# Attention ahead of a channel mix on one core: the second product of a head on quarters of TensorE, in whole float32

## The chip, the cores and the metric

One core of one Trainium2 chip runs the whole kernel. The metric is the device time of one execution in microseconds (us), the median of several runs.

## What is computed

Attention over 8 batches with 8 heads of 64, 576 queries, and keys and values averaged over pools of 8 (72 pooled keys); its output, put together to rows of 512, goes through a channel mix with a token shift.

```python
k_p = k.reshape(B, H, Sp, pool, D).mean(axis=3)      # Sp = 72, pool = 8, D = 64
v_p = v.reshape(B, H, Sp, pool, D).mean(axis=3)
scores = scale * np.matmul(q, k_p.transpose(0, 1, 3, 2))
attn = softmax(scores)
x = np.matmul(attn, v_p)                              # then (B, 576, 512)
x_prev = x one token earlier, zeros at a batch's start
xk = mu_k * x + (1.0 - mu_k) * x_prev                 # xr likewise with mu_r
k = np.maximum(xk @ w_k, 0.0)                         # 512 -> 1024
v = k * k @ w_v                                       # 1024 -> 512
r = 1.0 / (1.0 + np.exp(-(xr @ w_r)))                 # 512 -> 512
return (r * v).astype(np.float32)
```

The weights arrive as 64-bit floats, and the kernel makes float32 of them itself.

## The kernel before, in words

The 4608 tokens are 12 chunks of 384, and each chunk is three tiles of 128 tokens. A batch has 576 tokens, so chunks 1, 4, 7 and 10 lie over two batches, with 192 tokens of each; the other eight lie within one. `units` and `stretches` (L393) hold this.

For a tile, `softmax` (L676) makes the scores with 16 small matmuls (L698): 64 rows of the array by 64 columns, so that four of them, one on each quarter of the array, belong together. The softmax follows on DVE, ACT and POOL. In chunks 0 and 1 the weights of a tile are transposed by TensorE (`transposed` L813, `transposed_rest` L871); from chunk 2 on DVE turns blocks of 32 (`turned` L771), a DMA puts them in DRAM, and `fetch_turned` (L798) brings a chunk of them back, keys on the partitions, to the one buffer `turned_sb`.

`attended` (L901) is attention's second product. Two heads make a group g, four groups make a chunk. The 64 first keys of both heads lie on the 128 partitions; the values of both heads stand on the diagonal of one 128 x 128 matrix (`vbd_h`, `vbd_l`, made by `values` L616). But for chunk 0, whose product is in whole float32, weights and values are split into a rounded part and the rest (`pth`, `ptl`, made by `split_turned` L843 on ACT and DVE), and three matmuls give the product. A fourth, `ptr` with `vbd_r`, adds the 8 last keys. So a group is four matmuls of 384 columns, or eight of 192 where the chunk lies over two batches. Then the same thread makes the shifted rows: ACT writes `t` (L944), POOL copies one column from or to `carry` (L951, L953), and DVE makes `xm` (L964). A thread `x_parts` (L976), added at that point, splits `xm` on ACT (L980) and POOL (L982) into `xkh`, `xkl`, `xrh`, `xrl`.

`hidden` (L986) is the first layer: 8 output blocks of a chunk, each over four blocks of input `ct`, which are the four groups, with three matmuls each (one in chunk 0). `gate` (L1043) is the sigmoid's product, `mixed` (L1072) the last one: three tiles of 24 matmuls of 512 columns. `attended` of a chunk may begin when the gate of the chunk before it is done, so it stands among the matmuls of that chunk's `mixed`.

The order of all instructions is made when the program is written. Each piece of work is a generator that yields an engine and a planned length; the class `Order` holds a planned clock for each engine and takes, on the engine that can start first, the thread with the smallest due time. Due times come from the table `DUE`, found for this order, or from formulas. `LOADS` is the order of the first DMAs, and tables such as `SUM_BY`, `NORM_BY` and `LOW_BY` name the engine of sums over the pool, of the softmax's scaling and of the split of weights. A thread starts with the planned time 0:

```python
self.at, self.pe_at, self.step, self.last = 0.0, None, None, None
```

so a step of a thread that another thread adds midway can be planned earlier than the step that feeds it. Sums over the pool on POOL are three instructions at L578 (`halve`), on TensorE eight at L589 (`summed`).

Of the kernel before, what the change touches and what calls it, by code (L numbers as in the profile page):

```python
# [8 lines left out]
F32 = mybir.dt.float32  # L9
F32R = mybir.dt.float32r  # L10
# [35 lines left out]
SUM_BY = {"k0": "t", "k1": "v", "v0": "t", "v1": "t", "r0": "t", "k2": "t", "k3": "t", "v2": "g", "v3": "g", "r1": "v", "k5": "v", "k4": "v", "v5": "v", "r2": "v", "v4": "v"}

NORM_BY = {0: "v", 1: "v", 2: "v", 3: "v", 7: "g", 5: "g", 4: "v", 8: "v", 6: "v"}
WARMING = 4
# [1162 lines left out]
```

## Time and profile before

| | |
|---|---|
| median of 3 runs | 617.71 us (617.42 to 619.48) |
| the profiled execution | 618.18 us, span 616.3 us |
| mean granted clock of TensorE | 0.994 of full |
| PE busy | 600.9 us (97%) |
| DVE, ACT, POOL busy | 406.1, 359.6, 195.7 us |
| DMA | 68.73 MB, 37% of 16 engines' span |

The span is from the first to the last instruction; the execution's own time is 1.88 us longer. PE is the matrix engine, DVE the vector engine, ACT the scalar engine. The ends of matmuls are modelled, so the distance from one start to the next says more than a single duration. A product in whole float32 shows as two records in the trace, a split one as one record for each matmul.

### The profile page before, as it was taken

To read this page: it belongs to the slowest core of one execution; us is meant where nothing else is said; L and a number is where in the kernel's file an instruction comes from. 1 tells how busy PE (TensorE), PEld (TensorE's weight loads), DVE (VectorE), ACT (ScalarE), POOL (GpSimd) and SP (SyncE) were. 2 spreads that over 40 slices of the span, in tenths; PEclk is the share of its full clock that TensorE was granted. 3 is DMA by queue.
4 is the path that set the end of the run, shared out by engine and by line. 5 is a ranking of instruction groups with operands and counts; after the bars stand their busy time and mean duration, and the time that the engine had idled before them with its cause. 6 is when DMAs were issued, how large, how long until landed. Compare 5 with 4: busy or idle time off the path is not lost.

```text
span 616.3 us, 10622 instructions
## 1 busy us (share of the span) xinstructions
PE 600.9 (97%) x3948; PEld 509.3 (83%) x3948; DVE 406.1 (66%) x834; ACT 359.6 (58%) x761; POOL 195.7 (32%) x282
## 2 busy tenths in 40 slices
PE   7899999998999999999999999999999999999997
PEld 6755458887988988988988988988988988988985
DVE  5998969966766865984975854786885833623411
ACT  4999976764575766546646545665654643634420
POOL 1030373327205216425515105615523303304100
PEclk9999999999899999999999999999999999999999
DMA  9997122841358124156147123039215030000001
GB/s 293 394 360 233 43 89 77 204 155 52 77 182 199 45 81 105 60 163 167 36 178 178 54 70 95 19 131 225 68 40 130 19 78 34 18 1 35 18 1 51
DMA packets 59460, 68.73 MB, mean 112 GB/s; under 512 B 11664, under 2 KB 43664, under 8 KB 59408
## 3 DMA queue, kind: packets, MB, share of 16 engines
q1 hardware_dynamic: 59264, 67.91, 37.1%
q8 instruction: 31, 0.51, 0.4%
q14 instruction: 21, 0.17, 0.1%
q10 hardware_dynamic: 144, 0.13, 0.1%
HBM read 49.75 MB, written 18.28 MB: 110 GB/s over the span
## 4 chain that ended last, share of the span: by engine, by line
PE 87%; POOL 4%; DVE 3%; DMA 3%; ACT 2%; issue 1%; SPq 0%; DVEq 0%; POOLq 0%; ACTq 0%
PE mm L1092 31%; PE mm L1009 30%; PE mm L1061 17%; PE bank L938 5%; PE sc L698 3%; POOL stage L578 2%; DMA early_sl<-in_vm 1%; DMA stage<-in_vr 1%; POOL xkl L982 1%; POOL xrl L982 1%; ACT t L944 1%; PE mm L589 1%; DVE xm L964 1%; DVE sl L1037 1%; ACT xkh L980 1%
## 5 line engine op out<-in xcount | busy, mean ns | idle before, releaser
L1009 PE MATMUL mm<-xkh,w_k 128*128 128x384 f32 x704 | 182.4, 340 | 2.6 <-ACT xkh L980 2.6
L1092 PE MATMUL mm<-w_v,sh 128*128 128x512 f32 x528 | 170.3, 392 | 0.0
L1009 PEld LDWEIGHTS mm<-xkh,w_k 128*128 128x128 f32 x704 | 127.9, 190 | 4.4 <-ACT xkh L980 2.8
L1009 PE MATMUL mm<-xkl,w_k 128*128 128x384 f32 x352 | 119.3, 339 | 0.4
L1092 PEld LDWEIGHTS mm<-w_v,sh 128*128 128x128 f32 x528 | 99.2, 188 | 20.4
L1092 PE MATMUL mm<-w_v,sl 128*128 128x512 f32 x264 | 103.1, 390 | 0.0
L749 POOL TENSOR_TENSOR e<-e,sm 128x576 f32<-128x576 f32 x28 | 34.5, 1232 | 184.8 <-DVE sm L744 174.0
L944 ACT ACTIVATE t<-bank,om_sb 128x384 f32<-128x384 f32 x96 | 49.2, 580 | 61.0 <-PE bank L938 60.9
L1061 PE MATMUL mm<-w_r,xrh 128*128 128x512 f32 x264 | 84.0, 392 | 0.2 <-DVE rk L1029 0.2
L1035 ACT CAST sh<-rk 128x384 fp32r<-128x384 f32 x88 | 45.0, 513 | 62.7 <-DVE rk L1029 62.4
L964 DVE SCALAR_TENSOR_TENSOR xm<-bank,mu_sb,t 128x384 f32<-128x384 f32 x88 | 51.1, 612 | 39.7 <-POOL t L955 21.6
L1105 DVE TENSOR_TENSOR rs<-mm,rs 128x512 f32<-128x512 f32 (+1 forms) x37 | 24.8, 673 | 79.0 <-PE mm L1092 79.0
L1009 PEld LDWEIGHTS mm<-xkl,w_k 128*128 128x128 f32 x352 | 66.9, 190 | 1.9 <-POOL xkl L982 1.8
L1037 DVE TENSOR_TENSOR sl<-rk,sh 128x384 fp32r<-128x384 f32 x88 | 53.7, 612 | 19.8 <-ACT sh L1035 19.1
L982 POOL TENSOR_TENSOR xkl<-xm,xkh 128x384 fp32r<-128x384 f32 x44 | 45.8, 1041 | 65.0 <-ACT xkh L980 64.6
L1061 PEld LDWEIGHTS mm<-w_r,xrh 128*128 128x128 f32 x264 | 49.5, 188 | 11.0 <-DVE rk L1029 0.4
L1029 DVE SCALAR_TENSOR_TENSOR rk<-mm,rk 128x384 f32<-128x384 f32 x88 | 48.3, 549 | 13.7 <-ACT rk L1022 13.3
L1092 PEld LDWEIGHTS mm<-w_v,sl 128*128 128x128 f32 x264 | 49.6, 188 | 9.1
L1022 ACT ACTIVATE rk<-mm 128x384 f32<-128x384 f32 x88 | 43.0, 489 | 16.6 <-PE mm L1009 16.0
L1061 PE MATMUL mm<-w_r,xrl 128*128 128x512 f32 x132 | 51.5, 390 | 0.0
L982 POOL TENSOR_TENSOR xrl<-xm,xrh 128x384 fp32r<-128x384 f32 x44 | 45.6, 1036 | 2.3 <-ACT xrh L980 2.1
L578 POOL TENSOR_TENSOR stage<-stage 128x512 f32<-128x512 f32 (+5 forms) x51 | 43.5, 870 | 1.1
(126 smaller groups left out, 866.4 us busy)
## 6 DMA issues: line engine op xcount, KB each, us to landing
out<-rs SPq DMA_DIRECT2D x35, 256.0 KB, 2.0
passing<-pm SPq DMA_DIRECT2D x30, 288.0 KB, 2.8
qs<-in_qT SPq DMA_DIRECT2D x32, 256.0 KB, 4.2
stage<-in_kT SPq DMA_DIRECT2D x14, 576.0 KB, 4.7
turned_sb<-passing SPq DMA_DIRECT2D x40, 192.0 KB, 4.4
stage<-in_vm SPq DMA_DIRECT2D x14, 512.0 KB, 6.0
got_wk<-in_w_k SPq DMA_DIRECT2D x8, 512.0 KB, 9.1
got_wv<-in_w_v SPq DMA_DIRECT2D x8, 512.0 KB, 9.3
```

The source lines that it names most:

```text
L578: nc_eng.tensor_tensor(out=st[:, :, :w], in0=st[:, :, :w], in1=st[:, :, w:2 * w], op=ALU.add)
L749: eng.tensor_tensor(out=e, in0=e, in1=sm.broadcast_to([P, 2, 4, KEYS]), op=ALU.mult)
L944: nc.scalar.activation(out=t[:, m, 1:n + 1], in_=xp, func=AF.Copy, scale=om_sb[:, m, g:g + 1])
L964: nc.vector.scalar_tensor_tensor(out=xm[:, :n], in0=xp, scalar=mu_sb[:, m, g:g + 1], in1=t[:, m, :n], op0=ALU.mult, op1=ALU.add,)
L982: nc.gpsimd.tensor_tensor(out=lo, in0=xm[:, :n], in1=hi, op=ALU.subtract)
L1009: nc.tensor.matmul(out=hp, lhsT=w[:, o], rhs=x[:, ct, o_t], start=(ct == 0 and k == 0), stop=(ct == NCT - 1 and k == len(terms) - 1),)
L1022: nc.scalar.activation(out=rk[:, :n], in_=hp, func=AF.Relu)
L1029: nc.vector.scalar_tensor_tensor(out=rk[:, :n], in0=hp, scalar=0.0, in1=rk[:, :n], op0=ALU.max, op1=ALU.mult)
L1035: nc.scalar.copy(out=sh, in_=rk[:, :n])
L1037: nc.vector.tensor_tensor(out=operand("sl", c)[:, jt, o_t], in0=rk[:, :n], in1=sh, op=ALU.subtract)
L1061: nc.tensor.matmul(out=bank, lhsT=x[:, ct, o], rhs=w, start=(ct == 0 and k == 0), stop=(ct == NCT - 1 and k == len(terms) - 1),)
L1092: nc.tensor.matmul(out=bank, lhsT=s[:, o], rhs=w, start=(jt == 0 and k == 0), stop=(jt == NJT - 1 and k == len(terms) - 1),)
```

## The change

`attended` takes two groups at once (a, two in a chunk). The last keys' products come first, one on each of two banks. Then the 64 first keys follow without a split: for each of the four heads a matmul on one quarter of the array, 64 rows by 64 columns, weights and values in whole float32, added to the banks. From chunk 2 on TensorE reads the weights from the turned blocks directly. `split_turned` handles only the 8 last keys, for a whole chunk at once. What followed the product is a thread of its own, `shifted`, one for each group. The values are no longer put on a diagonal: `values` is one copy. There are two buffers of turned blocks, and heads 1 and 2 of each four change places in the layout.

The planner counts a change between whole and quarter matmuls (`CHANGE`), prefers on PE what stays in the present mode (`rank`, `STAY`), and starts an added thread at the time of what adds it. `DUE`, `LOADS` and the tables of engines are new.

```diff
 LOADS = (
-    "k0 k1 q0 wr3 q1 r0 q3 wk0 c0 q2 wk1 wv6 v1 k2 wk4 k3 q5 wv1 v0 wr2 wk3 wk2 v3 q4 wr0 v2 "
+    "k0 k1 q0 q2 q1 r0 c0 wk1 wk0 q4 q3 wr3 v0 k2 v1 wk4 wr2 v2 wv7 k3 q5 wk3 wk7 wr0 wk2 wv6 "
...
 DUE = {
-    "keys 0 0": 72.94, "values 0 0": -3.14, "keys 0 1": -79.49, "values 0 1": -66.31,
+    "keys 0 0": 360.51, "values 0 0": -73.7, "keys 0 1": -104.6, "values 0 1": 135.34,
...
+    CHANGE = {"quarters": 0.1, "whole": 0.25}
...
-        self.fresh.append(Thread(DUE.get(name, due), steps, spare, name))
+        t = Thread(DUE.get(name, due), steps, spare, name)
+        t.at = self.now
+        self.fresh.append(t)
...
+        stays = t.step[0] == "pe" and (t.step[3] if len(t.step) > 3 else "whole") == self.mode
+        return t.due - (STAY if stays else 0.0)
...
 def values(b, p):
-            nc.scalar.copy(out=(vbd_w if as_is else vbd_h[i])[r, gs, r], in_=o[r])
+        nc.scalar.copy(out=vs[b % 2][:, 2 * p:2 * p + 2], in_=o)
...
-    def split_turned(i):
+    def split_turned(c):
...
-        nc.scalar.copy(out=pt_h, in_=main)
-        nc.vector.tensor_tensor(out=pt_l, in0=main, in1=pt_h, op=ALU.subtract)
...
-    def attended(c, g, p):
+    def attended(c, a, p):
...
-        yield need(
-            "om", *[("rest", b) for b, *_ in segs],
-            *[("values" if as_is else "value parts", b, q) for b, *_ in segs for q in range(2)],
-        )
+        yield need("om", *[("rest", b) for b, *_ in segs], *[("values", b, a) for b, *_ in segs])
...
-        bank = yield take("bank")
-        t = yield take("t")
+        both = [(yield take("bank")), (yield take("bank"))]
...
-                vh, vl = vbd_h[i][:, g], vbd_l[i][:, g]
-                terms = [(vh, ph), (vl, ph), (vh, pl)]
-            terms.append((vbd_r[i][:, r, 2 * j:2 * j + 2, :], operand("ptr", c)[:, r, o]))
+        yield "pe", sum(2 * pe(k)[1] for _, _, k, _ in segs), False
...
+            for h2 in range(2):
                 nc.tensor.matmul(
+                    out=both[h2][:, at:at + k], lhsT=vbd_r[b % 2][:, a, 2 * h2:2 * h2 + 2, :],
+                    rhs=operand("ptr", c)[:, a, off + at:off + at + k], start=(q == 0), stop=False,
...
+        yield "pe", sum(pe(k, True)[1] for _, _, k, _ in segs), False, "quarters"
+        for q, (b, s, k, at) in enumerate(segs):
+            for j in range(2):
+                for h2 in range(2):
+                    r, to = slice(h2 * D, (h2 + 1) * D), both[h2][j * D:(j + 1) * D, at:at + k]
...
+                    nc.tensor.matmul(
+                        out=to, lhsT=vs[b % 2][r, 2 * a + j, :], rhs=pt, start=False, stop=True,
...
+        for h2 in range(2):
+            order.add(att_due[c] + 2 * a + h2, shifted(c, 2 * a + h2, p, both[h2]))
```

The order that comes of it is shown at three places. On PE, the last group of chunk 2 among the last matmuls of chunk 1's `mixed` (L1092, L1136 are `mixed`, `sc` are scores), before:

```order
L1092 MATMUL mm_118<-w_v_1135,sh_959 128x512
L938 MATMUL bank_117<-pth_1150,vbd_h_72 128x384
L938 MATMUL bank_117<-pth_1150,vbd_l_74 128x384
L938 MATMUL bank_117<-ptl_1151,vbd_h_72 128x384
L938 MATMUL bank_117<-ptr_1152,vbd_r_76 128x384
L698 MATMUL sc_114<-ks_69,qs_106 64x72 x16
L1009 MATMUL mm_119<-xkh_1330,w_k_540 128x384 x2
```

and now the last two groups of that chunk:

```order
L746 MATMUL sc_112<-ks_69,qs_106 64x72 x16
L956 MATMUL bank_114<-ptr_1119,vbd_r_74 128x384
L956 MATMUL bank_113<-ptr_1119,vbd_r_74 128x384
L972 MATMUL bank_114<-turned_99,vs_72 64x384
L972 MATMUL bank_113<-turned_99,vs_72 64x384
L972 MATMUL bank_114<-turned_99,vs_72 64x384
L972 MATMUL bank_113<-turned_99,vs_72 64x384
L1136 MATMUL mm_117<-w_v_1034,sh_920 128x512
L1136 MATMUL mm_117<-w_v_1034,sl_978 128x512
```

Four whole matmuls of one group are now two whole ones and four quarter ones of two groups. They begin a tile of `mixed`, with 24 matmuls of it behind them; before, the last group stood behind the last of them.

On POOL, the last column copies of chunk 2 and the sums of batch 2's values (`stage`), before:

```order
L982 TENSOR_TENSOR xkl_1331<-xm_84,xkh_1330 128x384
L982 TENSOR_TENSOR xrl_1340<-xm_83,xrh_1339 128x384
L578 TENSOR_TENSOR stage_110<-stage_110 128x2x256
L578 TENSOR_TENSOR stage_110<-stage_110 128x2x128
L578 TENSOR_TENSOR stage_110<-stage_110 128x2x64
L578 TENSOR_TENSOR stage_109<-stage_109 96x2x256
L578 TENSOR_TENSOR stage_109<-stage_109 96x2x128
L578 TENSOR_TENSOR stage_109<-stage_109 96x2x64
L578 TENSOR_TENSOR stage_108<-stage_108 128x2x256
L951 COPY t_81<-carry 128x2
L982 TENSOR_TENSOR xkl_1331<-xm_82,xkh_1330 128x384
```

and now:

```order
L1026 TENSOR_TENSOR xrl_1303<-xm_81,xrh_1302 128x384
L1026 TENSOR_TENSOR xkl_1285<-xm_80,xkh_1284 128x384
L650 TENSOR_TENSOR stage_108<-stage_108 128x2x256
L650 TENSOR_TENSOR stage_108<-stage_108 128x2x128
L650 TENSOR_TENSOR stage_108<-stage_108 128x2x64
L995 COPY t_78<-carry 128x2
L995 COPY t_79<-carry 128x2
L650 TENSOR_TENSOR stage_109<-stage_109 96x2x256
L650 TENSOR_TENSOR stage_109<-stage_109 96x2x128
L1026 TENSOR_TENSOR xkl_1285<-xm_81,xkh_1284 128x384
L1026 TENSOR_TENSOR xkl_1285<-xm_80,xkh_1284 128x384
```

Seven sums stood ahead of the last copy to `t`; now three stand ahead of the last two copies, and two behind them, ahead of the last two `xkl`.

On PE at the beginning, from the sums of the last value block that is waited for to the first layer, before:

```order
L589 MATMUL mm_118<-early_xrl,ident 128x128 x8
L938 MATMUL bank_117<-pth_287,rs_77 128x384
L938 MATMUL bank_117<-ptr_292,vbd_r_75 128x384
L938 MATMUL bank_115<-pth_287,rs_77 128x384
L938 MATMUL bank_115<-ptr_292,vbd_r_75 128x384
L1009 MATMUL mm_120<-xkh_454,got_wk_147 128x384
L938 MATMUL bank_116<-pth_287,rs_77 128x384
L938 MATMUL bank_116<-ptr_292,vbd_r_75 128x384
```

and now:

```order
L661 MATMUL mm_117<-early_xrl,ident 128x128 x4
L874 MATMUL bank_113<-ident,pm_87 128x128 x4
L746 MATMUL sc_112<-ks_69,qs_106 64x72 x16
L956 MATMUL bank_114<-ptr_250,vbd_r_73 128x384
L956 MATMUL bank_113<-ptr_250,vbd_r_73 128x384
L972 MATMUL bank_114<-pt_282,vs_71 64x384
L972 MATMUL bank_113<-pt_282,vs_71 64x384
L972 MATMUL bank_114<-pt_282,vs_71 64x384
L972 MATMUL bank_113<-pt_282,vs_71 64x384
L661 MATMUL mm_116<-turned_99,ident 128x144 x8
L1053 MATMUL mm_118<-xkh_432,got_wk_148 128x384
```

Before, the sum of `v0` (`early_xrl`) stood right ahead of the first group. Now `v0` (summed earlier, from `early_sl`) and `v1` (`early_xrl`) are both ahead of it, and the sum of `k3` (`turned`) stands between it and the first layer (`xkh`).

## Rows read from the trace of the kernel before

**Rows 1.** the page: span, share of the span by engine, chain of waits

```profile
span 616.3 us, 10622 instructions
PE 600.9 (97%) x3948; PEld 509.3 (83%) x3948; DVE 406.1 (66%) x834; ACT 359.6 (58%) x761; POOL 195.7 (32%) x282
...
PE 87%; POOL 4%; DVE 3%; DMA 3%; ACT 2%; issue 1%; SPq 0%; DVEq 0%; POOLq 0%; ACTq 0%
```

**Rows 2.** PE's waits: line, whom for, us in total, times, longest

```profile
PE mm L1009 <- ACT xkh L980: 2.6, 1, 2.6
```

**Rows 3.** stretches of the span: busy us by engine, granted clock, DMA share, GB/s

```profile
16.00:32.00 16.00, 13.17 (x149) 11.22 (x147) 14.68 (x34) 14.55 (x48) 0.00 (x0) 1.00 1.05 389
...
140.00:180.00 40.00, 37.32 (x289) 33.01 (x288) 26.66 (x55) 23.92 (x46) 15.81 (x19) 0.91 0.29 74
```

**Rows 4.** PE in order of time round 150 us: start, us, instruction, idle before

```profile
152.12 1.01 PE L1009 MATMUL mm<-xkh,w_k 128*128 128x384 f32 x2 [2.60 <-ACT xkh L980]
...
158.17 0.41 PE L1009 MATMUL mm<-xkl,w_k 128*128 128x384 f32 x1
158.42 0.52 PE L1009 MATMUL mm<-xkh,w_k 128*128 128x384 f32 x2
158.77 0.33 PE L1009 MATMUL mm<-xkl,w_k 128*128 128x384 f32 x1
```

**Rows 5.** POOL in order of time, the same stretch

```profile
144.24 6.44 POOL L578 TENSOR_TENSOR stage<-stage 128x512 f32<-128x512 f32 x7
150.62 0.25 POOL L951 COPY t<-carry 128x2 f32<-128x2 f32 x1
152.14 1.01 POOL L982 TENSOR_TENSOR xkl<-xm,xkh 128x384 fp32r<-128x384 f32 x1 [1.28 <-ACT xkh L980]
```

**Rows 6.** ACT in order of time, the same stretch

```profile
143.40 1.05 ACT L944 ACTIVATE t<-bank,om_sb 128x384 f32<-128x384 f32 x2 [0.66 <-PE bank L938]
```

**Rows 7.** PE, the second product of a chunk within one batch

```profile
325.11 0.34 PE L938 MATMUL bank<-pth,vbd_l 128*128 128x384 f32 x1
...
326.17 0.34 PE L938 MATMUL bank<-ptr,vbd_r 96*128 96x384 f32 x1
```

**Rows 8.** PE, the second product of a chunk over two batches

```profile
79.32 0.28 PE L938 MATMUL bank<-ptl,vbd_h 128*128 128x192 f32 x1
...
79.99 0.27 PE L938 MATMUL bank<-pth,vbd_h 128*128 128x192 f32 x1
```

**Rows 9.** PE, whole float32 products of 384 columns, chunk 0

```profile
40.30 6.72 PE L1009 MATMUL mm<-xkh,got_wk 128*128 128x384 f32 x20
```

**Rows 10.** PE, the scores of one tile between whole products

```profile
318.34 0.39 PE L1061 MATMUL mm<-w_r,xrh 128*128 128x512 f32 x1
318.66 0.73 PE L698 MATMUL sc<-ks,qs 64*64 64x72 f32 x32
319.32 0.50 PE L1092 MATMUL mm<-w_v,sh 128*128 128x512 f32 x1
319.66 0.40 PE L1092 MATMUL mm<-w_v,sl 128*128 128x512 f32 x1
```

**Rows 11.** PE, the scores of the tile that spans two batches

```profile
34.73 0.73 PE L698 MATMUL sc<-ks,qs 64*64 64x72 f32 x32
35.39 0.91 PE L1009 MATMUL mm<-xkh,got_wk 128*128 128x384 f32 x2
```

**Rows 12.** PE, the beginning: sums of values, second product, first layer, gate

```profile
19.44 4.01 PE L589 MATMUL mm<-early_sl,ident 128*128 128x128 f32 x32 [0.96 <-DMA early_sl<-in_vm]
...
27.11 1.98 PE L589 MATMUL mm<-early_xrl,ident 128*128 128x128 f32 x16
29.71 0.91 PE L938 MATMUL bank<-pth,rs 128*128 128x384 f32 x2 [0.62 <-ACT rs L627]
...
33.07 0.91 PE L1009 MATMUL mm<-xkh,got_wk 128*128 128x384 f32 x2 [1.44 <-DVE xkh L964]
...
59.29 4.46 PE L1061 MATMUL mm<-got_wr,xrh 128*128 128x512 f32 x10
```

More of the change, by code (lines that the diff above doesn't have):

```diff
@@ L156, in __init__ @@
         self.table = "exp"
+        self.mode = "whole"
         self.slow, self.bursts = True, []
@@ L248, in run @@
             eng = t.step[0]
-            at, t = min((c for c in starts if c[1].step[0] == eng and c[0] <= first + 0.1), key=lambda c: c[1].due)
+            at, t = min((c for c in starts if c[1].step[0] == eng and c[0] <= first + 0.1), key=self.rank)
             self.ready.remove(t)
             _, length, lock, *func = t.step
-            if func and func[0] and func[0] != self.table:
+            if eng == "pe":
+                mode = func[0] if func else "whole"
+                if mode != self.mode:
+                    length, self.mode = length + self.CHANGE[mode], mode
+                length = self.stretch(at, length)
+            elif func and func[0] and func[0] != self.table:
                 length, self.table = length + 1.3, func[0]
-            if eng == "pe":
-                length = self.stretch(at, length)
             self.free[eng] = at + length
@@ L325, in attention_then_channel_mix @@
     ks = [const.tile([P, NPAIR, KEYS], F32, name=f"ks{i}") for i in range(2)]
-    vbd_h = [const.tile([P, NPAIR, P], F32R, name=f"vbd_h{i}") for i in range(2)]
-    vbd_l = [const.tile([P, NPAIR, P], F32R, name=f"vbd_l{i}") for i in range(2)]
+    vs = [const.tile([P, NPAIR, D], F32, name=f"vs{i}") for i in range(2)]
     vbd_r = [const.tile([REM, 2, 4, D], F32R, name=f"vbd_r{i}") for i in range(2)]
@@ L344, in operand @@
         if (kind, c) not in operands:
-            dtype = F32 if kind != "ptr" and whole(c, USED_BY[kind[:-1].rstrip("t")]) else F32R
+            dtype = F32 if kind == "pt" or kind != "ptr" and whole(c, USED_BY[kind[:-1]]) else F32R
             operands[kind, c] = sb.tile(shapes[kind], dtype, name=f"{kind}_{c}", tag=kind)
@@ L363, in attention_then_channel_mix @@
         order.give("w", i)
-    turned_sb = const.tile([P, CH // BLOCK, 6 * BLOCK], F32, name="turned_sb")
+    turned_sb = [const.tile([P, CH // BLOCK, 6 * BLOCK], F32, name=f"turned{i}") for i in range(2)]
     for i in range(4):
-        order.give("tmp", turned_sb.rearrange("p a n -> p (a n)")[:, i * WP:(i + 1) * WP])
+        order.give("tmp", turned_sb[0].rearrange("p a n -> p (a n)")[:, i * WP:(i + 1) * WP])
     passed = ctx.enter_context(tc.tile_pool(name="passed", bufs=1, space=bass.MemoryType.DRAM))
@@ L372, in attention_then_channel_mix @@
     early = {}
-    for tag, n in (("sl", 2), ("ptl", 1), ("xrl", 1)):
-        t = sb.tile([P, n, 2 * POOL * KEYS], F32, name=f"early_{tag}", tag=tag)
+    for tag, n in (("sl", 2), ("xrl", 1), ("turned", 2)):
+        if tag == "turned":
+            t = turned_sb[1].rearrange("p a n -> p (a n)").rearrange("p (i n) -> p i n", i=n)
+        else:
+            t = sb.tile([P, n, 2 * POOL * KEYS], F32, name=f"early_{tag}", tag=tag)
         for i in range(n):
@@ L429, in constants @@
         order.make("ident")
-        yield "dve", 0.5, False
-        nc.vector.memset(vbd_w, 0.0)
-        order.make(("values clear", 0))
-        for t in (vbd_h[1], vbd_l[1]):
-            yield "pool", 0.5, False
-            nc.gpsimd.memset(t.bitcast(F32), 0.0)
-        order.make(("values clear", 1))
     def warm():
@@ L616, in values @@
     def values(b, p):
-        i = b % 2
-        as_is = b == 0 and whole(0, "p")
-        yield need(("v", 2 * b + p), ("attended", last_chunk[b - 2]) if b > 1 else ("values clear", b))
+        yield need(("v", 2 * b + p), *([("attended", last_chunk[b - 2])] if b > 1 else []))
         if not b:
@@ L795, in free_turned, with free_second @@
         yield need(*[("full", kind, i) for kind, n in (("k", NJT), ("r", NCT), ("v", NJT)) for i in range(n)])
-        order.give("turned", turned_sb)
+        order.give("turned", turned_sb[0])
+    def free_second():
+        yield need(("early", "turned", 0), ("early", "turned", 1))
+        order.give("turned", turned_sb[1])
     def fetch_turned(c):
@@ L816, in transposed @@
         yield need(("pm", i), *([("attended", c - 1)] if c else []))
-        if not whole(c, "p"):
-            yield need(("early", "ptl", 0))
         got, pm = held.pop(("pm", i))
@@ L830, in transposed @@
         yield act(NPAIR * P)
-        if whole(c, "p"):
-            nc.scalar.copy(out=operand("pth", c)[:, :, o], in_=tp)
-        else:
-            pt_h, pt_l = operand("pth", c), operand("ptl", c)
-            nc.scalar.copy(out=pt_h[:, :, o], in_=tp)
-            yield dve(NPAIR * P, False)
-            nc.vector.tensor_tensor(
-                out=pt_l[:, :, o], in0=tp, in1=pt_h[:, :, o], op=ALU.subtract
-            )
+        nc.scalar.copy(out=operand("pt", c)[:, :, o], in_=tp)
         order.give("bank", bank)
@@ L867, in split_turned, with turned_done @@
-        if not left:
-            order.give("turned", whole_d)
-        order.make(("side", i))
+        order.make(("split", c))
+    def turned_done(c):
+        yield need(("attended", c))
+        order.give("turned", held.pop(("turned", c)))
     def transposed_rest(c, first, n):
@@ L921, in attended, with shifted @@
+        order.count(("attended", c), 2 * len(parts[c]))
+        for h2 in range(2):
+            order.add(att_due[c] + 2 * a + h2, shifted(c, 2 * a + h2, p, both[h2]))
+    def shifted(c, g, p, bank):
+        off, n = parts[c][p]
+        segs = stretches(starts[c] + off, n)
         t = yield take("t")
-        order.make(("attending", c, g, p))
         xp = bank[:, :n]
-        r, j = g // 2, g % 2
-        yield "pe", sum(
-            (pe(k, True)[1] + pe(k)[1] if as_is else pe(k, False, 4)[1]) for _, _, k, _ in segs
-        ), False
@@ L941, in attended @@
-        order.count(("attended", c), NPAIR * len(parts[c]))
         yield "act", 2 * (act(n)[1] + 0.05), False
@@ L1150, in attention_then_channel_mix @@
     order.add(-5, free_turned())
+    order.add(-5, free_second())
     for c, n in enumerate(CHUNKS):
```

144 lines of the change are left out of this document (59 added, 85 removed), and 181 rows, old and new, of the table DUE.

## The prediction

> **What bounds the kernel now.** I read the page first. PE is busy for 600.9 of 616.3 us, and the chain of waits lies on PE for 87% [rows 1]. So DVE, at 66%, and ACT, at 58%, can be relieved without any gain where PE has work; what counts is PE's own work, its waits, and the beginning, where it is fed late. Then I read PE's waits: the longest is one of 2.6 us in the first layer, ended by ACT's `xkh` [rows 2], and the table of stretches shows a granted clock of 0.91 in the 40 us that hold it [rows 3]. Third, that place in order of time. ACT began the last group's `t` of chunk 2 at 143.40 and needed 1.05 us [rows 6]. The copy of one column that completes it stood behind seven sums of values on POOL, from 144.24, and ran at 150.62 [rows 5]. PE went on at 152.12, at half speed, until 158.42 [rows 4]. Last, PE's steady state and its beginning, for the prices below.
>
> **PE's own work.** Starts of split matmuls of 384 columns lie (326.17 - 325.11) / 6 = 0.177 us apart [rows 7], of 192 columns (79.99 - 79.32) / 6 = 0.112 [rows 8]. A whole float32 matmul of 384 columns is two records: 20 of them took 6.72 us, the last 0.49 of it modelled tail, so (6.72 - 0.49) / 19 = 0.328 each and 0.656 for the pair [rows 9].
>
> What a quarter costs, only the scores show: 16 quarter matmuls of 72 columns, 32 records. One after the other at the pace of rows 9 they would take 16 x 0.656 x 72 / 384 = 1.97 us; four at a time 0.49. From their start to that of the next whole matmul it is 319.32 - 318.66 = 0.66 [rows 10]. So four do run at a time. It is also 0.66 (35.39 - 34.73) in the tile over two batches, where the column halves of the array read different keys [rows 11], which is what the new matmuls do throughout. Four quarters of 384 columns, a wave, should thus take 0.656.
>
> The change to quarters and back has a price. From the last whole matmul ahead of the scores to the second behind them it is 319.66 - 318.34 = 1.32 us; two whole matmuls of 512 columns take 2 x 0.177 x 512 / 384 = 0.47 of it and the quarters 0.49, so **0.36 us** remain for one excursion [rows 10].
>
> Now the sums. Seven chunks from chunk 2 on lie within one batch, and three over two; chunk 1 is of the second kind too.
> - Within one batch: twelve split matmuls (12 x 0.177 = 2.12) give way to two waves (1.31): -0.81, seven times: -5.7.
> - Over two batches: twenty-four of 192 columns (2.69) give way to four waves of 192 (1.31): -1.38, three times: -4.1.
> - The matmuls of the last keys stay, in number and size.
> - Excursions: the order has 35 stretches of quarter matmuls before and 53 now. Of the 24 new groups of quarters six stand beside scores and share theirs; in chunks 2 to 11 it is 14 that don't: 14 x 0.36 = +5.0.
>
> **Chunks 2 to 11 together: -4.8 us.** Much of what the arithmetic gives goes back in excursions.
>
> TensorE now reads weights out of turned blocks, in runs of 32 columns. The nearest rows are sums over the pool that read runs of 64 and 72: 4.01 us for 32 records of 136 columns on average, at most 0.125 each, where 0.328 x 136 / 384 = 0.116 is the full pace [rows 12]. That is at most 0.0045 a run, or 0.11 a wave of 384 columns and 2.2 us in all. I take 0, since 4.01 includes the last record's tail, and keep +2.2 as a bound.
>
> **The beginning.** `v0` was the last value block to come: its sum ran at 27.11, the first group at 29.71, the first layer began at 33.07 and the gate at 59.29 [rows 12]. The first pair of groups now needs `v0` only, and by the list of first loads and the sizes of their tiles `v0` comes with 4.99 MB instead of 8.26 MB; `v1` came with 5.25 MB before, and the row that waits for it starts at 19.44. But PE's order still has `k2` and `v1` ahead of the first group, and `k3`, which comes with 8.79 MB, a little more than `v0` did, behind it and ahead of the first layer: so its sum can't begin before about 28.5, and takes some 1.2. The first layer then starts near 30.5: -2.5. Chunk 0's product gives 4 x 0.656 - 2 x 0.656 = 1.3 and pays two excursions: -0.6. Chunk 1 gives 1.38 and pays two: -0.7. Together **-3.8**. DVE and ACT, busy for 14.68 and 14.55 of 16 us there [rows 3], lose work too (the splits of values and of weights), so that they shouldn't take over; but `wk2` now stands 25th in the list, so its conversion could eat all of this. Bounds: 0 and -7.
>
> **The stall in chunk 2.** It cost 2.6 us of idling. After it 18 matmuls from 152.12 to 158.42 took 6.30 us instead of 18 x 0.177 = 3.19: 3.1 lost to the clock, at the lower of its two levels, 1.2 instead of 2.4 GHz [rows 4]. In the new order three sums stand ahead of the last two copies, and the last pair of groups has 24 matmuls of `mixed` behind it, 24 x 0.236 = 5.7 us, and a tile of scores. Sums ahead of the copies: at most 6.44 / 7 = 0.92 each, 2.8. So **-5.7**. The cause lies in the planner: before, a thread that another one added started at planned time 0, so its conversion could be planned before `xm` existed; now it starts when it is added. The bound on the other side: the same stall elsewhere, 0 instead of -5.7.
>
> On DVE, ACT and POOL I cost the rest at nothing: fewer instructions (no `ptl`, no `vbd_l`, three instead of nine for the last keys of a chunk), all under PE. POOL gets more scaling of early tiles; it was idle from 16 to 32 us [rows 3]. With the cover gone, each would count with its own duration.
>
> **Sum** against the profiled execution: 618.18 - 4.8 - 3.8 - 5.7 = **603.9 us**. That execution lies 0.47 above the median of the runs, 617.71, well inside their spread; I keep 603.9.
>
> **Rivals.**
> - *The quarters overlap less in long streams.* In the scores 0.66 includes the price of the change. Were it no fixed price but a pace, a wave would take 0.656 x 0.66 / 0.49 = 0.88; there are 24 waves of 384 columns' worth in the kernel (two in chunk 0, two in each other): 24 x 0.23 = +5.5, time 609.4. For: no row shows a long quarter. Against: rows 10 and 11 fit a fixed price. The Trainium skill (TensorE: Matmul & The Clock Gate, Part 3, on packing small matmuls) has a rule against the change: it gives four matmuls on four row strips as 3.07 times as fast as one after the other, not four times. By that ratio a wave would take 0.656 x 4 / 3.07 = 0.855 and the kernel 608.7, an estimate from that page; the rows above stand nearer to four than to three.
> - *The stall stays*, in chunk 2 or at another boundary, because sums on POOL still stand between copies: +5.7, time 609.6. For: the two sums behind the copies and ahead of `xkl`. Against: the slack worked out above.
> - *The second pair comes too late* at the chunk boundaries. Before, one group alone was left at the end; now two are, and on ACT alone `t` takes 2 x 1.05 [rows 6]; then from the copy to the matmul 152.12 - 150.62 = 1.50, and two or three POOL subtractions of 1.01 [rows 4, 5]: 2.1 + 1.5 + 3 = 6.6 us, against 5.7 for the 24 matmuls and some 1.9 until the fourth input block is read. The margin is 1 us, and sums of 2 to 3 us stand on POOL in the same place in five chunks. If the margin fails with a stall of the present size, 5.7, three boundaries undo the gain: 603.9 + 3 x 5.7 = **621.0, slower**. It decides from 14 us in ten boundaries on.
> - *Nothing comes of the beginning, and both dearer waves and a stall come*: 603.9 + 3.8 + 5.5 + 5.7 = 618.9, no change.
>
> **Chances.** The forecast, from 600.7 (the beginning at -7) to 609.9 (the beginning at 0 and the runs of 32 at +2.2): 0.62. Dearer waves: 0.11. The stall stays: 0.11. The second pair too late: 0.09. No change: 0.07. The range from 597.5 to 612 holds the first three, with some 2 to 3 us on either side for small waits that come or go in the new order, and leaves out the last two. A measurement of this kernel tells about 0.3% (1.9 us) from no change; faster by more than that has 0.62 + 0.11 + 0.11 = 0.84, within it 0.07, slower 0.09.
>
> **What would show it.** A wave of four long quarters: next start 0.65 behind the first if right, 0.85 or more if the first rival holds. No wait of over 1 us on PE after 100 us, and a granted clock of 1.00 in all stretches there. The gate's first matmul near 55.5. The forecast is wrong if PE's idle time grows, if excursions cost over 0.6, or if the gate begins no earlier than 59.

## The result, and the profile after

| | before | after |
|---|---|---|
| median of 4 runs | 618.18 us (617.42 to 619.48) | 608.05 us (607.31 to 608.88) |
| ratio | | 0.9826, 95% interval 0.9801 to 0.9851 |
| the profiled execution | 618.18 us | 608.31 us, span 606.5 us |

Faster by 10.1 us, where the terms of the forecast add up to 14.3; the time is 4.2 us above the forecast of 603.9 and within its range. The page of the kernel after, the lines that answer to [rows 1]:

```profile
span 606.5 us, 10538 instructions
...
PE 594.3 (98%) x4018; PEld 489.9 (81%) x4018; DVE 370.5 (61%) x742; ACT 326.2 (54%) x650; POOL 206.4 (34%) x293
...
PE 81%; DMA 10%; DVE 2%; ACT 2%; POOL 2%; SPq 1%; issue 1%; DVEq 0%; POOLq 0%; ACTq 0%
```

DVE and ACT are relieved by 36 and 33 us, and that is not where the gain is: PE's own work and waits are. Of the chain, 10% now lie on DMA, which had 3%. The table of stretches, answering to [rows 3] (140 to 180 us, then 16 to 32):

```profile
140.00:180.00 40.00, 40.00 (x319) 34.89 (x318) 30.02 (x64) 23.21 (x44) 15.52 (x19) 1.00 0.54 154
16.00:32.00 16.00, 15.08 (x173) 12.98 (x172) 14.68 (x33) 13.18 (x31) 6.68 (x11) 1.00 1.03 403
```

The stall in chunk 2 is gone: PE is busy for all of 40 us, at full clock. But in the beginning DVE is busy for 14.68 of 16 us, exactly as before. PE there, answering to [rows 12]:

```profile
28.62 0.88 PE L972 MATMUL bank<-pt,vs 64*64 64x384 f32 x8
29.42 2.23 PE L661 MATMUL mm<-turned,ident 128*128 128x144 f32 x16
31.68 1.56 PE L1053 MATMUL mm<-xkh,got_wk 128*128 128x384 f32 x4
...
38.16 1.56 PE L1053 MATMUL mm<-xkh,got_wk 128*128 128x384 f32 x4 [1.32 <-DVE xkh L1008]
...
59.48 2.74 PE L1105 MATMUL mm<-got_wr,xrh 128*128 128x512 f32 x6
```

The first layer starts at 31.68 instead of 33.07, but the gate at 59.48, no earlier than before: one of the three signs that the prediction named for being wrong did come, in this execution. The granted clock differs too, ahead of these rows. Here it was 0.5, the lower of the two levels, from 11.46 to 14.87 us; in the profiled execution of before it was 1.00 up to the stall (the same two us, after and before):

```profile
12.00:14.00 2.00, 2.00 (x11) 2.00 (x11) 1.66 (x5) 0.90 (x2) 0.15 (x1) 0.50 1.19 308
```

```profile
12.00:14.00 2.00, 2.00 (x20) 2.00 (x20) 1.67 (x7) 1.33 (x7) 0.00 (x0) 1.00 1.12 330
```

And PE's waits have a new entry besides loads and `xkh`:

```profile
PE mm L1053 <- DVE xkh L1008: 1.3, 1, 1.3
PE sc L746 <- DMA qs<-in_qT: 1.2, 3, 0.6
...
PE mm L1136 <- DVE w_v L642: 1.1, 1, 1.1
```

It stands in chunk 1's last product; further on, a wave of the second product by itself (eight records, then the next whole matmul):

```profile
126.67 0.39 PE L1136 MATMUL mm<-w_v,sl 128*128 128x512 f32 x1
128.18 0.73 PE L1136 MATMUL mm<-w_v,sh 128*128 128x512 f32 x2 [1.12 <-DVE w_v L642]
...
138.51 0.88 PE L972 MATMUL bank<-turned,vs 64*64 64x384 f32 x8
139.32 0.50 PE L1136 MATMUL mm<-w_v,sh 128*128 128x512 f32 x1
```

Split by stage, from the starts of PE's rows: up to the first `xkl` matmul of chunk 1's first layer 96.78 before and 95.87 after, -0.9 (forecast -3.8). From there to the last matmul 515.3 and 506.5, -8.8 (forecast -4.8 - 5.7 = -10.5).

### The profile page after: what moved, and what is told of

It reads as the page before. It is cut to its first block, busy times and chain, and to the rows that moved or that the text cites. A ratio compares the mean times of both kernels' runs of the same rounds, so it can differ in the third digit from the quotient of the medians.

```text
span 606.5 us, 10538 instructions
## 1 busy us (share of the span) xinstructions
PE 594.3 (98%) x4018; PEld 489.9 (81%) x4018; DVE 370.5 (61%) x742; ACT 326.2 (54%) x650; POOL 206.4 (34%) x293
## 4 chain that ended last, share of the span: by engine, by line
PE 81%; DMA 10%; DVE 2%; ACT 2%; POOL 2%; SPq 1%; issue 1%; DVEq 0%; POOLq 0%; ACTq 0%
PE mm L1136 32%; PE mm L1053 26%; PE mm L1105 15%; DMA qs<-in_qT 3%; PE sc L746 3%; PE bank L972 3%; DMA got_wr<-in_w_r 2%; DMA got_wv<-in_w_v 2%; DMA stage<-in_vm 2%; PE bank L956 1%; DMA turned<-passing 1%; POOL stage L650 1%; ACT e L770 1%; SPq L857 0%; DVE mx L761 0%
## 5 line engine op out<-in xcount | busy, mean ns | idle before, releaser
L1053 PE MATMUL mm<-xkh,w_k 128*128 128x384 f32 x704 | 180.0, 336 | 0.3 <-DVE rk L1073 0.3
L1136 PE MATMUL mm<-w_v,sh 128*128 128x512 f32 x528 | 172.1, 396 | 1.1 <-DVE w_v L642 1.1
L1053 PEld LDWEIGHTS mm<-xkh,w_k 128*128 128x128 f32 x704 | 126.6, 188 | 2.2 <-DVE rk L1073 1.0
L1136 PEld LDWEIGHTS mm<-w_v,sh 128*128 128x128 f32 x528 | 99.0, 188 | 29.8 <-issue 7.1
L1053 PE MATMUL mm<-xkl,w_k 128*128 128x384 f32 x352 | 117.7, 334 | 0.0
L1136 PE MATMUL mm<-w_v,sl 128*128 128x512 f32 x264 | 103.1, 390 | 0.0
L797 POOL TENSOR_TENSOR e<-e,sm 128x576 f32<-128x576 f32 x30 | 36.7, 1223 | 137.6 <-DVE sm L792 127.1
L1073 DVE SCALAR_TENSOR_TENSOR rk<-mm,rk 128x384 f32<-128x384 f32 x88 | 48.4, 554 | 36.2 <-ACT rk L1066 35.7
L1081 DVE TENSOR_TENSOR sl<-rk,sh 128x384 fp32r<-128x384 f32 x88 | 49.9, 576 | 16.9 <-ACT sh L1079 15.9
L1105 PEld LDWEIGHTS mm<-w_r,xrh 128*128 128x128 f32 x264 | 49.6, 188 | 10.8 <-DVE rk L1073 0.2
L1136 PEld LDWEIGHTS mm<-w_v,sl 128*128 128x128 f32 x264 | 49.6, 188 | 9.3
L650 POOL TENSOR_TENSOR stage<-stage 128x512 f32<-128x512 f32 (+8 forms) x54 | 47.3, 880 | 2.0
```

What stands on the lines that cost most here:

```text
L650: nc_eng.tensor_tensor(out=st[:, :, :w], in0=st[:, :, :w], in1=st[:, :, w:2 * w], op=ALU.add)
L797: eng.tensor_tensor(out=e, in0=e, in1=sm.broadcast_to([P, 2, 4, KEYS]), op=ALU.mult)
L1053: nc.tensor.matmul(out=hp, lhsT=w[:, o], rhs=x[:, ct, o_t], start=(ct == 0 and k == 0), stop=(ct == NCT - 1 and k == len(terms) - 1),)
L1073: nc.vector.scalar_tensor_tensor(out=rk[:, :n], in0=hp, scalar=0.0, in1=rk[:, :n], op0=ALU.max, op1=ALU.mult)
L1081: nc.vector.tensor_tensor(out=operand("sl", c)[:, jt, o_t], in0=rk[:, :n], in1=sh, op=ALU.subtract)
L1105: nc.tensor.matmul(out=bank, lhsT=x[:, ct, o], rhs=w, start=(ct == 0 and k == 0), stop=(ct == NCT - 1 and k == len(terms) - 1),)
```

## The experiments

**The stall in chunk 2: three kernels made from the one before.** First the planner's rule alone:

```diff
-        self.fresh.append(Thread(DUE.get(name, due), steps, spare, name))
+        t = Thread(DUE.get(name, due), steps, spare, name)
+        t.at = self.now
+        self.fresh.append(t)
```

> The kernel before with one thing of the change alone: a thread that another one adds starts at the planned time of what adds it. Theory of the prediction (this start time was the cause of the stall in chunk 2): the 2.6 us of idling and the 3.1 us at the lower clock go, ratio to before near 612.5 / 618.2 = 0.991. Rival (the cause is the sums of values on POOL ahead of the last copy, and the start time does not decide their place): in the order that comes of it nine sums stand ahead of the last copy instead of seven, so a wait of 2.6 us or more stays on PE in the first layer of chunk 2, ratio 0.999 to 1.005.

618.66 us, ratio 1.0015 (0.9999 to 1.0032): nothing gained. PE in chunk 2, and the stretch:

```profile
152.01 0.73 PE L700 MATMUL sc<-ks,qs 64*64 64x72 f32 x32 [1.67 <-DVE e L733]
154.06 0.62 PE L1011 MATMUL mm<-xkh,w_k 128*128 128x384 f32 x2 [1.32 <-ACT xkh L982]
155.24 0.69 PE L1011 MATMUL mm<-xkl,w_k 128*128 128x384 f32 x1 [0.56 <-POOL xkl L984]
```

```profile
140.00:180.00 40.00, 35.96 (x304) 31.63 (x306) 31.56 (x67) 21.97 (x46) 18.37 (x21) 0.91 0.42 121
```

The wait is only cut in three, together longer than the 2.60 of before, and the clock is at 0.91 as before. So the start time 0, the cause that the prediction gave, does not make the stall by itself. The sums ahead of the copy were next. (They are sums of batch 3's values and last keys; the words ahead of the order rows and the prediction's second step call them batch 2's or only values.) Once they were made to wait:

```diff
 def values(b, p):
+        if b == 3:
+            yield need(("shifting", 2, NPAIR - 1, 0))
...
 def last_values(b):
+        if b == 3:
+            yield need(("shifting", 2, NPAIR - 1, 0))
```

> The kernel before, where the threads of batch 3's values and of its last keys wait for the last column copy of chunk 2, so that the sums on POOL come behind it; PE's order is the same until then. If these sums were the cause of the stall: no wait over 1 us on PE between 140 and 180 us, granted clock 1.00 there, 5.7 us less, ratio near 0.991. If the stall has another cause (ACT's or DVE's own work), the wait stays and the ratio is 1.00. If the sums only move on and hold up the next chunk's beginning, the wait comes back later and the ratio is 0.995 to 1.00.

620.97 us, ratio 1.0053 (1.0034 to 1.0071): slower. In chunk 2 PE idled for 0.5 us; the stall came back at the start of chunk 3:

```profile
197.55 1.01 PE L1013 MATMUL mm<-xkh,w_k 128*128 128x384 f32 x2 [1.99 <-ACT xkh L984]
199.27 0.69 PE L1013 MATMUL mm<-xkl,w_k 128*128 128x384 f32 x1 [0.70 <-POOL xkl L986]
```

```profile
180.00:240.00 60.00, 57.23 (x414) 49.59 (x413) 46.41 (x98) 31.99 (x62) 19.87 (x32) 0.94 0.47 125
```

Then the sums of the two value blocks given to DVE:

```diff
-"r2": "v", "v4": "v"}
+"r2": "v", "v4": "v", "v6": "v", "v7": "v"}
```

> The kernel before, where the sums of batch 3's two value blocks are made by DVE instead of POOL; the three sums of its last keys stay on POOL (two of them ahead of the last copy). If the sums on POOL were the cause: the wait of 2.6 us and the lower clock go, ratio near 0.991, as where the sums wait. If DVE, which then has six sums more, becomes the one that is late: a wait of 1 to 3 us stays, ratio 0.995 to 1.00.

615.91 us, ratio 0.9964 (0.9951 to 0.9977). The long wait and the lower clock are gone, yet a third of 5.7 us is all that was won:

```profile
150.78 0.44 PE L1009 MATMUL mm<-xkl,w_k 128*128 128x384 f32 x1 [0.47 <-POOL xkl L982]
158.53 0.62 PE L1009 MATMUL mm<-xkh,w_k 128*128 128x384 f32 x2 [0.71 <-DVE rk L1029]
```

```profile
140.00:180.00 40.00, 38.83 (x305) 33.57 (x304) 32.85 (x67) 24.02 (x48) 13.26 (x14) 1.00 0.38 109
```

1.2 us of idling are left in this stretch, and 0.9 at the start of chunk 3. The three together: the sums did make the long wait, but where they are moved away, other waits come at the same boundary or at the next one. Something else in the changed kernel gives the slack, and the place of the last pair of groups was the candidate. So in the changed kernel that pair was put behind:

```diff
+        if a and c == 2:
+            yield need(("mixing", c - 1, CHUNKS[c - 1] // P - 1))
...
-    "attended 2 1 0": -166.35
+    "attended 2 1 0": -1000.0
```

> The changed kernel, where the second pair of groups of chunk 2 may begin only when the last tile of chunk 1's last product has; in the order that comes of it the pair stands behind the first 18 matmuls of chunk 2's first layer, instead of ahead of 24 matmuls of the last product. Theory (the stall is gone because of the matmuls that stand behind the pair, which cover ACT's, DVE's and POOL's work on it, 6.6 us): 18 matmuls from there on and a tile of scores cover 3.9 us, so a wait of 2 to 4 us on PE comes back in the first layer of chunk 2 with a lower clock behind it, 5 to 8 us in all, ratio to before 0.991 to 0.996. Rival (the place of the sums on POOL made the stall, the place of the pair is of no account): no wait over 1 us, ratio 0.983.

613.57 us, ratio 0.9937 (0.9917 to 0.9956), 5.5 us above the changed kernel: about as much as the stall was put at. In the trace the pair stands behind nine matmuls of the first layer, with nine more and a tile of scores behind it, where the expectation has 18 ahead of it. PE in chunk 2, and the stretch:

```profile
150.76 0.61 PE L1055 MATMUL mm<-xkh,w_k 128*128 128x384 f32 x2 [1.44 <-ACT xkh L1026]
152.38 0.44 PE L1055 MATMUL mm<-xkl,w_k 128*128 128x384 f32 x1 [1.02 <-POOL xkl L1028]
...
169.29 0.50 PE L1107 MATMUL mm<-w_r,xrh 128*128 128x512 f32 x1 [1.53 <-DVE rk L1075]
```

```profile
140.00:180.00 40.00, 35.91 (x324) 30.28 (x323) 32.03 (x68) 22.88 (x42) 18.70 (x21) 1.00 0.51 147
```

The waits are there, on ACT, POOL and DVE in turn, 4.0 us in all. In one point the expectation missed: in this execution the granted clock stayed at 1.00. Not all of the 5.5 us is the pair's: the wait for `w_v` in chunk 1, which the changed kernel has too, is 0.7 us longer here, and there is one excursion more. In the eight executions of this kernel the mean granted clock was 0.988 to 1.000 and the time 617.55 to 612.50 us, so the clock does fall in others of them. So with the pair late, waits come back: PE needs the 24 matmuls of the last product that it has left when the pair is through. That these alone would have sufficed, with all seven sums still ahead of the copy, no run shows. In the changed kernel POOL still has sums ahead of the copies and behind them, and nobody waits for it:

```profile
138.40 2.63 POOL L650 TENSOR_TENSOR stage<-stage 128x512 f32<-128x512 f32 x3
140.96 0.31 POOL L995 COPY t<-carry 128x2 f32<-128x2 f32 x2
141.22 2.11 POOL L650 TENSOR_TENSOR stage<-stage 96x512 f32<-96x512 f32 x2
```

**The price of a wave.** The changed kernel with each quarter matmul issued twice:

```diff
+                    for again in range(2):
-                    nc.tensor.matmul(
+                        nc.tensor.matmul(
```

> The changed kernel with every quarter matmul of the second product issued twice, so the part of the 64 first keys counts double in the output; no other instruction moves. There are 24 waves' worth of 384 columns. Theory (a wave is 0.656 us and the price of an excursion is fixed): 24 x 0.656 = 15.7 us more than the changed kernel, 608.1 + 15.7 = 623.8, ratio to before 1.009. Rival of the prediction (0.88 us a wave): 21.1 more, 629.2, ratio 1.018.

624.52 us (621.67 to 626.62), 16.5 above the changed kernel, where 15.7 were expected. The total is weak evidence: its runs spread over 5 us, and the profiled one, the slowest, has a wait of 3.34 us for `w_v` (1.12 in the changed kernel) with a lower clock from it on. A doubled wave by itself is better:

```profile
144.86 1.54 PE L973 MATMUL bank<-turned,vs 64*64 64x384 f32 x16
146.33 0.50 PE L1137 MATMUL mm<-w_v,sh 128*128 128x512 f32 x1
```

146.33 - 144.86 = 1.47 us, against 139.32 - 138.51 = 0.81 for the single one above: a wave is 0.66 us and 0.15 are fixed. The single one, 0.81, lay between the prediction's two signs, 0.65 and 0.85; only the doubling tells. The forecast's 0.656 holds, the rival's 0.88 doesn't. That is four quarters at a time; the Trainium skill (TensorE: Matmul & The Clock Gate, Part 3) gives 3.07 times for four row strips, by which it would be 0.855, an estimate, and the measurement decides for four on these quarters. The turned blocks, read in runs of 32, cost nothing: the groups of eight by themselves took 0.81 (one 0.76), 28.62 to 29.42 among them, where the weights are not turned.

**The price of an excursion.** In the chunks over two batches, whole and quarter matmuls alternating by batch:

```diff
-        for q, (b, s, k, at) in enumerate(segs):
-            for h2 in range(2):
-                nc.tensor.matmul(
-                    out=both[h2][:, at:at + k], lhsT=vbd_r[b % 2][:, a, 2 * h2:2 * h2 + 2, :],
...
         yield "pe", sum(pe(k, True)[1] for _, _, k, _ in segs), False, "quarters"
         for q, (b, s, k, at) in enumerate(segs):
+            for h2 in range(2):
+                nc.tensor.matmul(
+                    out=both[h2][:, at:at + k], lhsT=vbd_r[b % 2][:, a, 2 * h2:2 * h2 + 2, :],
...
             for j in range(2):
```

> The changed kernel; in the four chunks that lie over two batches the whole and the quarter matmuls of the second product alternate by batch, which adds one excursion to quarters and back to each of eight pairs of groups and changes nothing else on any engine. Theory (0.36 us an excursion): 8 x 0.36 = 2.9 us more than the changed kernel, 611.0 us, ratio to before 0.9872; in the trace a group of quarters of these chunks takes 0.33 + 0.15 us from its first start to the next whole matmul. Rivals: 0.1 us an excursion (0.8 more, ratio 0.984), 0.6 us (4.8 more, ratio 0.990).

610.58 us, ratio 0.9894 (0.9869 to 0.9920); 2.5 above the changed kernel, forecast 2.9. The trace has nine more stretches of quarters, 62 against 53, where eight were meant. One pair of groups in chunk 4, in this kernel and in the changed one:

```profile
226.11 0.36 PE L957 MATMUL bank<-ptr,vbd_r 96*128 96x192 f32 x2
226.40 0.56 PE L971 MATMUL bank<-turned,vs 64*64 64x192 f32 x8
226.89 0.47 PE L957 MATMUL bank<-ptr,vbd_r 96*128 96x192 f32 x2
227.29 0.56 PE L971 MATMUL bank<-turned,vs 64*64 64x192 f32 x8
227.77 0.50 PE L1135 MATMUL mm<-w_v,sh 128*128 128x512 f32 x1
```

```profile
226.29 0.59 PE L956 MATMUL bank<-ptr,vbd_r 96*128 96x192 f32 x4
226.81 0.88 PE L972 MATMUL bank<-turned,vs 64*64 64x192 f32 x16
227.62 0.50 PE L1136 MATMUL mm<-w_v,sh 128*128 128x512 f32 x1
```

From the first whole matmul to the one behind, 1.66 us against 1.33: one more excursion is 0.33 us for the same work, where 0.36 was taken. The Trainium skill (TensorEngine Tiling, Key Properties) says that a change of tiling mode drains TensorE, and gives no price; here it has one.

**The small waits.** DVE in the changed kernel ahead of the wait at 128.18:

```profile
122.13 0.20 DVE L829 STREAM_TRANSPOSE pm<-e 128x64 f32<-128x64 f32 x1
125.79 0.95 DVE L894 TENSOR_TENSOR ptr<-turned,ptr 32x768 fp32r<-32x768 f32 x1 [3.46 <-ACT ptr L892]
126.77 0.76 DVE L761 TENSOR_REDUCE mx<-sc 128x8 f32<-128x576 f32 x1
127.45 0.68 DVE L642 TENSOR_TENSOR w_v<-got_wv,w_v 128x512 fp32r<-128x512 f32 x1
```

DVE stood idle for 3.46 us, because its next instruction waited, through ACT, for turned weights from DRAM, and the split of `w_v` stood behind it. That DVE keeps its order the Trainium skill says too (Perfetto Trace Analysis, Per-engine timelines). The edit:

```diff
-        (nc.vector if v else nc.gpsimd).tensor_tensor(
+        (nc.vector if v and (kind, i) != ("v", 5) else nc.gpsimd).tensor_tensor(
```

> The changed kernel with the subtraction that makes the low part of block 5 of w_v on POOL instead of DVE, at the same place of the program; nothing else moves. In the trace of the changed kernel PE waited for this subtraction at 128.18 us; DVE had it behind an instruction that waits, through ACT, for the turned weights of chunk 2 from DRAM, and was idle for 3.46 us. Theory (DVE's order holds it up, not its work): that wait is gone, the last product's tile runs through, and the gate of chunk 2 and all that follows come 1.2 to 1.4 us earlier; time 606.8. Rival (POOL's instructions in its place are late instead, or another operand of that matmul is as late): a wait of 0.5 us or more stays there.

605.86 us (2 runs). POOL did it from 117.93 to 119.5, seven us ahead of need, and PE runs through:

```profile
127.20 0.39 PE L1136 MATMUL mm<-w_v,sl 128*128 128x512 f32 x1
127.43 0.39 PE L1136 MATMUL mm<-w_v,sh 128*128 128x512 f32 x1
127.66 0.51 PE L956 MATMUL bank<-ptr,vbd_r 96*128 96x384 f32 x2
```

From chunk 1's first layer to the end it is 503.9 us instead of 506.5; 1.3 of these 2.6 are the wait itself (from start to start, 1.51 less 0.23), most of the rest are waits for `qs` and in first layers that became shorter. Next, the load for which ACT waited:

```diff
+SWAPPED = {('r', 1): ('v', 4), ('v', 4): ('r', 1)}
...
+            k, j = SWAPPED.get((kind[1], i), (kind[1], i))
...
-                in_=sources[kind[1]][:, i * WP:(i + 1) * WP].bitcast(I32),
+                in_=sources[k][:, j * WP:(j + 1) * WP].bitcast(I32),
```

The exchange is made where the load is issued, so that the planner's view and all other instructions stay.

> The changed kernel with the first load of block 1 of w_r and that of block 4 of w_v in each other's places in the queue of loads (29th and 36th instruction of SP); nothing else moves. In the trace of the changed kernel ACT waited 1.50 us for block 1 of w_r until 49.56, and two of PE's waits at 53.0 and 55.6 us, 0.37 and 0.39, were for ACT's or DVE's work behind it. Theory (ACT, held by that load, holds the first layer): the load lands some 6 us earlier, ACT's wait and both of PE's go, the gate begins 0.7 us earlier, near 58.8. Rival (ACT's exponents by head, behind it, hold the first layer by themselves): the gate moves by less than 0.3.

606.64 us (2 runs); ACT no longer waits for the load, the gate begins at 58.61, and from the first layer to the gate it is 27.07 us instead of 27.81. But the kernel of the experiment before, with the old place of the load, has 27.11 here, without a wait for it: in five executions of the unchanged queue ACT waited 1.50, 1.22, 0.99, 0.81 and 0 us, and went on at 49.56, 48.88, 48.45, 48.77 and 48.54. So the load lands within some 1.1 us, and the rest is when ACT comes to it. So this run shows little more than that the wait can be removed. Both edits together:

> The changed kernel with both small edits at once: the low part of block 5 of w_v on POOL, and the first loads of block 1 of w_r and block 4 of w_v in each other's places. Theory (the wait of 1.28 us for w_v and ACT's wait for w_r are separate): 1.3 to 2.2 us from the first (the run with it alone had 605.86 us, its part from chunk 1's first layer on was 2.6 us shorter) and 0 to 0.9 from the second (the gate at 58.61 with it; 58.34 to 59.48 without it, as the load lands by itself sooner or later), so 605.3 us, ratio to before 0.979. Rival (the single looks were chance): the changed kernel's own 608.1, ratio 0.983.

605.04 us (604.63 to 605.82), ratio 0.9786 (0.9772 to 0.9801). That is 3.0 us under the changed kernel, and the runs don't overlap: this version beats both.

**The beginning.** PE waits 1.3 us near 38 us for the second pair's `xkh` in every one of these. First, the conversion of `w_k`'s block 7, which stands ahead of it on ACT and DVE, put later:

```diff
+        if (kind, i) == ("k", 7):
+            yield need(("x", 0, 3, 0, 0))
```

> The changed kernel, where the conversion of block 7 of w_k (one step of ACT, three of DVE), which the first layer reads last, may begin only when the last input block of chunk 0 is made; the order of the engines changes from there on. In five executions of the changed order PE waited 1.3 us near 38 us for the second pair's first input block. Theory (DVE's and ACT's conversions ahead of it are what that block waits for): it comes some 1 us earlier, the wait is under 0.5 us, and the gate begins 0.8 us or more after a shorter first layer: 26.3 us from the first layer's start to the gate instead of 27.1 to 27.8. Rival (ACT's exponents by head of tile 3 hold it alone): the wait stays above 1 us and the distance is 27 or more. The time itself: 606.5 to 608, not to be told from the changed kernel unless the new order brings waits of its own.

633.14 us, ratio 1.0255 (1.0228 to 1.0282). The wait fell to 0.83 us, but the layer then waited 1.26 and 0.50 for `sh`, so that it took 29.2 us to the gate, and far behind it the tables no longer fit their order:

```profile
111.68 1.24 PE L748 MATMUL sc<-ks,qs 64*64 64x72 f32 x32 [4.46 <-DVE e L781]
...
121.58 0.69 PE L1055 MATMUL mm<-xkh,w_k 128*128 128x384 f32 x1 [3.28 <-ACT w_k L641]
```

An inconclusive test, then: the order moved with the edit. The second one keeps every place and leaves out work:

```diff
+        left_out = (kind, i) == ("k", 7)
...
+        if not left_out:
             nc.scalar.activation(out=ff, in_=top.bitcast(F32), func=AF.Abs, scale=DOWN)
...
+            if not left_out:
                 nc.vector.tensor_scalar(
...
+        if not left_out:
             nc.vector.tensor_scalar(out=t, in0=t, scalar1=3, scalar2=None, op0=ALU.logical_shift_left)
```

> The kernel with both small edits, and of the conversion of block 7 of w_k one step on ACT (0.56 us of its time) and two on DVE (0.86) are left out, so that block 7's weights are wrong; all else keeps its place. These steps stand on both engines right ahead of the second pair's t and of its first input block, for which PE waited 1.3 us near 38 us in every execution of this order. Theory (the conversions on DVE and ACT hold the first layer, since both engines are full there): the wait falls to 0.6 us or less, and from the first layer's start to the gate it is 26.1 to 26.5 us instead of 27.1; time near 604.3. Rival (what is won there is lost at the next wait of the layer, for sh): the distance stays at 26.8 or more. Rival (POOL's column copies hold it): the wait stays above 1 us.

604.88 us, no different from 605.04. PE:

```profile
36.31 1.56 PE L1059 MATMUL mm<-xkh,got_wk 128*128 128x384 f32 x4 [0.40 <-DVE xkh L1014]
...
40.14 0.73 PE L752 MATMUL sc<-ks,qs 64*64 64x72 f32 x32 [0.54 <-DVE e L785]
```

The wait fell from 1.31 to 0.40, so the conversions on ACT and DVE hold that block. But 0.54 came back as a wait for DVE four us later, and from the first layer to the gate it is 26.64 us, 0.43 less, between theory and rival. So the first layer runs against the work of these two engines in more than one place; a step of each was left out, and the run does not tell them apart.

**The planner's rule in the new order.** Undone in the changed kernel:

```diff
-        t.at = self.now
```

> The changed kernel without the planner's new rule: an added thread starts at the planned time 0 again; the tables stay. Rival to the view that the rule is what the order needs: the first experiment showed no gain from it in the old order (ratio 1.0015). If it is worth nothing here either, ratio 0.983. If planned starts before the threads exist put conversions and copies in wrong places, waits on PE come back at the chunk boundaries, 2 us or more in all, ratio 0.986 to 0.995. I take the second as likelier, as the tables were made for the rule.

667.20 us, ratio 1.0778 (1.0749 to 1.0806). PE's two longest sums of waits:

```profile
PE mm L1052 <- DVE rk L1072: 11.5, 9, 3.6
PE mm L1052 <- DVE rs L1148: 7.1, 6, 3.5
```

Neither theory had the size. Alone the rule gives nothing; without it the new tables, which were made for it, lose 59 us. Due times and rule belong together, and neither can be priced by taking it out.

## Why the prediction was right, and where it was off

- **A wave 0.656, an excursion 0.36.** Right: 0.66 by doubling, 0.33 by one more excursion. So is the count: from chunk 1's first layer on there are 42 stretches of quarter matmuls, 14 more than before. That the -4.8 us hold follows from these prices; the sum further below leaves 0.2 us.
- **The stall, -5.7.** Right in size for the two profiled executions, wrong in the cause that it gave. The clock is at 1.00 in all stretches from 60 us to the end of the last full one, as said; of the waits after 100 us one, for `w_v`, is over 1 us (1.12). But the sentence that the cause lies in the planner's start time fell: with that alone the stall stays, ratio 1.0015. The step that carried, as the prediction had it too, is the 24 matmuls behind the last pair; with the pair late the kernel is 5.5 us slower. No run prices the stall by itself. The 3.1 us of it that are the clock's belong to the profiled execution: of 47 other executions of the kernel before, the sixteen with its mean granted clock, 0.994, took 618.04 us in the mean, the ten with 0.997 took 617.37. Less of the lower clock was worth 0.7 us there; where in them the clock fell is not on record. The third rival (the second pair too late) named the right mechanism, and the margin held.
- **The beginning, -3.8: the term that was mis-sized.** It gave 0.9 in these two executions. Two steps of it failed. The sum of `k3` was said to take some 1.2 us; it is 16 records, and the 32 of [rows 12] took 4.01, so 2.0; its row shows 2.23 with the modelled tail, from 29.42 instead of 28.5, and the first layer starts at 31.68 instead of 30.5. And the sentence that DVE and ACT, relieved, shouldn't take over was wrong: DVE is as full as before, and the second pair's `xkh` comes 1.32 us late behind its and ACT's conversions; later waits for `sh` are 0.37 and 0.39. The gate was forecast 25.0 us behind the first layer; it came 27.8 behind.
- **Part of that miss is the execution.** The profiled execution of before had an early beginning. In four executions of its order (it, and the first three experiments) the first layer starts at 33.07, 34.45, 35.14 and 34.72, the first `xkl` matmul of chunk 1 at 96.78, 97.67, 97.75 and 97.70. In the changed order the first layer starts at 31.68, 31.07 and 32.25 (the kernel itself, the late pair, the split on POOL), that `xkl` at 95.87, 94.73 and 95.74. By the means the first layer gains 2.7 us, about the -2.5 of the forecast, and the beginning as a whole 2.0; 1.8 of the first layer's gain goes back until the gate. The clock may be part of it: a stretch at 0.5, ahead of 23 us, stands in the three experiments of the old order and in the first and third of the changed one, and not in the two whose first layer is earliest, 33.07 and 31.07. No run varied it by itself.
- **Small waits, not in the sum: +1.9.** From chunk 1 on, before has some 1.5 us of them outside the stall, the changed kernel 3.4, counted by distances of starts beyond the usual (as idle time of the page, 0.6 and 2.05); the one for `w_v` is the largest. The forecast had only a margin for them. With -4.8, -5.7 and +1.9 the later part comes to -8.6; the traces show -8.8.
- The range and the side were right because the two larger terms were priced from rows, the stall's with a wrong cause beside the right one; the weakest term was the one with the widest bounds, 0 to -7.

## What to carry to other kernels

Price a new shape of instruction as a pace, from the nearest rows, and a fixed price; then issue the work twice, and add a change by itself: the two came apart that way, and both held. The stall at this boundary was a lack of slack: ask what PE still has to do when the last late operand is issued, and lengthen that, before moving work between the engines that take turns in being late. And DVE, idle for 3.46 us behind a DMA, held up a split that did not need it; moving that split to an idle engine, all else in place, won 2 us, while two small edits that made the planner order everything anew cost 25 and 59.

## What was not expected of the hardware

- The clock did not follow the idle time alone. It fell within single waits of 2.60 us [rows 2, 4], of 1.99 (the sums that wait) and of 3.34 (the doubled waves), and at the third of 1.67, 1.32 and 0.56 close together; it stayed at 1.00 with 1.44 and 1.02 close together, and with 1.80 us by itself (both with the pair put late).
- Nor is it the same in every execution of one kernel: the mean granted clock of 47 executions of the kernel before lay between 0.991 and 1.000.
- The same queue of first loads and the same order begin differently in each execution: one load landed between some 48.4 and 49.6, the wait for it was 0 to 1.5 us, and the first layer began between 31.07 and 32.25. A gain of less than 1 us in the beginning can't be read from a single trace.
